# An attention stage that feeds a gated MLP and a second MLP, on one core: query transfers a tile earlier, eight weight conversions moved into attention, mismatch products by column parts, copies dealt out anew

## The chip, the cores and the metric

The kernel runs on one core of a Trainium2 chip. The metric is the device time of one execution in microseconds. Engines are named as in the profile: PE is the matrix engine (PEld its weight loads), DVE, ACT and POOL the vector, scalar and general engines, SP the engine that issues most transfers. Every engine takes its own instructions in order.

## The reference, cut to what matters

```python
# attention, B=2, H=8, S=768, D=64; 6 sign bits of q @ proj and k @ proj give a bucket
q_bits = (q @ proj) > 0 ; k_bits = (k @ proj) > 0
mask   = bucket(q)[..., :, None] == bucket(k)[..., None, :]
scores = where(mask, (q @ k.T) / sqrt(D), -1e9)
attn   = softmax(scores) ; x = (attn @ v) laid out as [B, S, H*D]        # 512 wide
# first MLP
h = relu(x @ w_in) ; u, v = halves(h)                                    # w_in 512 x 1024
v = layernorm(v) ; g = u * (w_spatial @ v + b_spatial)                   # w_spatial 768 x 768
x = g @ w_out                                                            # w_out 512 x 512
# second MLP
out = x + relu((layernorm(x) * g_ln) @ w_ch1) @ w_ch2                    # 512 x 2048, 2048 x 512
```

The weights w_in, w_out, w_ch1 and w_ch2 arrive as 64-bit floats, two 32-bit words to a number.

## The kernel before, in words

**Attention** walks 96 tiles, in the order batch, head, group, tile: a tile is 128 queries against all 768 keys of one head, two tiles make a group, three groups a head, two heads a pair. `attn_step(i)` issues the transposes of tile i, the scores of tile i+2, the maximum (DVE, line 310) and the exponential (ACT, line 323) of tile i+1, and, at each second tile, the product with the values (`weighted`, line 351) of the group that ended two tiles ago. The transposed exponentials leave PSUM in two halves `e`: half c=0 is copied by ACT (line 340), half c=1 by DVE (line 342). `weighted` writes 64 output columns at a time, in turn to the upper and the lower half of the partitions.

**Per pair**, `pair_load` brings raw keys and queries, `mismatch` multiplies them with the signs' projection (PE, line 245, four products of 384 columns with a full 128-wide weight, two instructions each) and DVE turns the sums into mask rows `m` (line 246, two instructions); `pair_split` splits keys and queries into a high and a low part on POOL and DVE; `head_prep` (keys) and `group_prep` (queries) call `passes_of`, which lets SP copy the parts and the mask rows from SBUF to SBUF into the operand tiles `ks` and `qs` (lines 269, 270, 275). These five stand at 10, 7, 6, 4 and 0 tiles ahead of their pair (`AT`); `group_prep` stands `QA` = 3 tiles and one step ahead of its group, with `QB` = 3 buffers.

**Conversion of weights** (`stage_f64`, `words_f64`, `join_f64`, `split_f64`): a 512 KB load issued from ACT's queue, one ACT instruction (line 102), five on DVE (103 to 107), one on POOL (111), and then the split into a high part on ACT (80) and a low part on POOL (86). Twelve such pieces (w_out, then both halves of w_in) are converted during attention at the tiles `CONV_AT`, and stored to DRAM by `kept` for a second use. The other 32 pieces (`w1_piece`, `w2_piece`, sixteen each, names f_w, w1t, w2t) are converted after attention by `load_f64`.

**The first MLP**, `moe1(b)`, runs for batch 0 from tile 60 of attention on, in between the tiles, and for batch 1 after attention, where the list `fill` hangs steps of the second MLP between its steps: pieces 0 to 4 of w1 and w2, layer norms, and `second(0)` to `second(4)`. The rest of the pieces (5 to 15) comes after, two a step of `second`.

**Order.** The order of instructions on each engine is made by the planner of the framework, from a simulated timeline; `tc.issue_after(...)` ties a step to an instruction that must have been issued before it. What the program's order says is thus a start, not the order on the chip.

## Time and profile before

| what | value |
|---|---|
| median of 3 runs | 737.61 us (737.4 to 738.12) |
| the profiled execution's own time | 737.13 us |
| its span, first to last instruction | 734.9 us |
| PE busy | 686.0 us (93%) |
| DVE busy | 438.7 us (60%) |
| ACT busy | 303.6 us (41%) |
| POOL busy | 190.9 us (26%) |
| mean DMA rate | 115 GB/s, 84.37 MB |

How to read it: the shares are means over stages. The profile's own table by slices shows DVE near 90% in the first quarter of the span and again late in the third, and near 15% in the last fifth. The execution that the profile shows took 2.2 us more than its span, and 0.5 us less than the median of the runs.

### The profile page before, as it was taken

What the parts mean: (1) busy time and instruction counts of PE and PEld (TensorE: products, weight loads), DVE (VectorE), ACT (ScalarE), POOL (GpSimd) and SP (SyncE); (2) the same over time, 40 slices, a digit from 0 to 9 for tenths busy, and PEclk for the clock granted to TensorE, in tenths of its full rate; (3) what the DMA queues carried; (4) which work ended last, traced back from release to release, by engine and by line L of the source; (5) the groups of instructions that cost most, each with busy time, mean ns of one, the idle gap of its engine ahead of it and who ended that gap; (6) DMA issues with size and microseconds to landing.
All of it is one profiled execution on the core that took longest, in us unless ns stands there. A gap on an engine that the chain in (4) does not pass through costs nothing.

```text
span 734.9 us, 9990 instructions
## 1 busy us (share of the span) xinstructions
PE 686.0 (93%) x3580; PEld 533.1 (73%) x3580; DVE 438.7 (60%) x849; ACT 303.6 (41%) x583; POOL 190.9 (26%) x182
## 2 busy tenths in 40 slices
PE   6999999898999999998889999799988999999997
PEld 5767667675767777776678887587766788888885
DVE  3698987897665645444798459676899712112112
ACT  2676766685556545344364222453323201100100
POOL 2234143334352222110144243244544400000000
PEclk8899999999999999999999999899999999999999
DMA  6765866674554554212625153523232101001001
GB/s 168 187 159 155 248 163 179 207 195 122 156 175 98 178 179 102 80 38 72 220 62 197 44 165 122 199 90 114 89 112 86 58 1 57 1 0 58 1 0 58
DMA packets 51922, 84.37 MB, mean 115 GB/s; under 512 B 6970, under 2 KB 36206, under 8 KB 50850
## 3 DMA queue, kind: packets, MB, share of 16 engines
q1 hardware_dynamic: 38834, 54.37, 25.8%
q10 hardware_dynamic: 13040, 29.36, 12.3%
q8 instruction: 29, 0.48, 0.3%
q14 instruction: 19, 0.16, 0.1%
HBM read 51.12 MB, written 12.58 MB: 87 GB/s over the span
## 4 chain that ended last, share of the span: by engine, by line
PE 60%; DVE 15%; DMA 11%; ACT 4%; issue 4%; POOL 3%; SPq 1%; DVEq 0%; ACTq 0%; POOLq 0%
PE acc L747 12%; PE pc L437 11%; PE sc L299 7%; DMA f_w<-in_w 7%; PE pv L437 7%; PE pt L337 6%; PE pg L607 6%; PE po L351 6%; PE py L437 3%; POOL f64c_w L111 2%; DVE f_w L105 2%; DVE x L310 2%; DMA qs<-q 2%; DMA f_v<-in_w_in 1%; DVE f64c_w L107 1%
## 5 line engine op out<-in xcount | busy, mean ns | idle before, releaser
L747 PE MATMUL acc<-w2t,ch 128*128 128x512 f32 x576 | 145.3, 398 | 6.6 <-DVE ch L738 5.2
L437 PE MATMUL pc<-xh,w1t 128*128 128x512 f32 x576 | 146.9, 400 | 3.9 <-DVE xh L731 2.7
L747 PEld LDWEIGHTS acc<-w2t,ch 128*128 128x128 f32 x576 | 107.5, 189 | 34.5 <-DVE ch L738 8.1
L437 PEld LDWEIGHTS pc<-xh,w1t 128*128 128x128 f32 x576 | 110.0, 192 | 30.0 <-ACT f64c_w L102 2.9
L310 DVE TENSOR_SCALAR_CACHE_REDUCE x<-sc 128x768 f32<-128x768 f32 x96 | 89.5, 950 | 23.1 <-PE sc L299 22.9
L323 ACT ACTIVATE x<-x,nb 128x768 f32<-128x768 f32 x96 | 89.3, 931 | 32.7 <-DVE x L310 32.6
L738 DVE SCALAR_TENSOR_TENSOR ch<-pc,ch 128x512 fp32r<-128x512 f32 x48 | 33.0, 688 | 112.6 <-ACT ch L737 112.6
L299 PE MATMUL sc<-ks,qs 128*128 128x512 f32 (+3 forms) x384 | 86.3, 363 | 9.2 <-PE po L351 3.1
L337 PE MATMUL pt<-ident,x 128*128 128x128 f32 x576 | 79.8, 278 | 9.8 <-ACT x L323 9.3
L337 PEld LDWEIGHTS pt<-ident,x 128*128 128x128 f32 x576 | 67.6, 143 | 26.7 <-ACT x L323 17.6
L737 ACT ACTIVATE ch<-pc 128x512 fp32r<-128x512 f32 x48 | 28.5, 593 | 131.5 <-PE pc L437 131.5
L299 PEld LDWEIGHTS sc<-ks,qs 128*128 128x128 f32 (+1 forms) x384 | 59.8, 199 | 21.6 <-PE po L351 6.2
L351 PE MATMUL po<-e,vv 128*64 128x256 f32 x576 | 74.1, 393 | 0.4 <-DVE m L246 0.4
L111 POOL TENSOR_TENSOR f64c_w<-f_w,f64c_w 128x512 f32<-128x512 f32 x32 | 43.7, 1368 | 93.9 <-DVE f64c_w L107 77.9
L340 ACT ACTIVATE e<-pt 128x384 f32<-128x384 f32 x96 | 46.5, 488 | 45.4 <-PE pt L337 44.5
L342 DVE COPY e<-pt 128x384 f32<-128x384 f32 x96 | 52.7, 549 | 20.7 <-PE pt L337 20.2
L351 PEld LDWEIGHTS po<-e,vv 128*64 128x64 f32 x576 | 37.5, 138 | 24.4 <-issue 7.3
L102 ACT ACTIVATE f64c_w<-f_w 128x512 f32<-128x512 f32 x32 | 21.4, 669 | 63.0 <-DMA f_w<-in_w 59.6
L607 PE MATMUL pg<-vn,w_sp 128*128 128x512 f32 x180 | 44.1, 397 | 0.0
L437 PE MATMUL pv<-w_u,act_x 128*128 128x512 f32 x144 | 37.8, 398 | 4.7 <-DMA w_u<-ws_u 2.8
L607 PEld LDWEIGHTS pg<-vn,w_sp 128*128 128x128 f32 x180 | 33.3, 188 | 7.6
L437 PE MATMUL py<-w_out,act_g 128*128 128x512 f32 x144 | 35.8, 396 | 2.1 <-ACT act_g L426 2.1
(131 smaller groups left out, 813.3 us busy)
## 6 DMA issues: line engine op xcount, KB each, us to landing
f_w<-in_w ACTq DMA_DIRECT2D x32, 512.0 KB
ks<-k SPq DMA_DIRECT2D x48, 192.0 KB
qs<-q SPq DMA_DIRECT2D x144, 64.0 KB
wst_sp<-in_w_spT SPq DMA_DIRECT2D x12, 384.0 KB
w_out<-ws_out SPq DMA_DIRECT2D x2, 2048.0 KB
vv<-in_v SPq DMA_DIRECT2D x16, 192.0 KB
ot<-y_dram SPq DMA_DIRECT2D x12, 256.0 KB
out<-ot SPq DMA_DIRECT2D x12, 256.0 KB
```

The costliest lines, as they stand in the source:

```text
L111: nc.gpsimd.tensor_tensor(cf, tf, cf, op=ALU.add)
L299: nc.tensor.matmul(sc[:, csl], qs[:rows, i, qsl], ks[:rows, i, csl], start=(i == 0), stop=(i == 1))
L310: last["max"] = nc.vector.tensor_scalar(x, t["sc"], MASKED, FMAX, op0=ALU.min, op1=ALU.min, accum_out=nb,).ins
L323: last["exp"] = nc.scalar.activation(t["x"], t["x"], AF.Exp, bias=t["nb"], scale=-1.0, accum_out=z_sum[b][:, n, h : h + 1]).ins
L337: nc.tensor.transpose(pt[:, i, :], t["x"][:, kt * P : (kt + 1) * P], ident)
L340: nc.scalar.activation(e, pt, AF.Copy)
L342: nc.vector.tensor_copy(e, pt)
L351: nc.tensor.matmul(po[a : a + D, :GW], heads[b, h]["vv"][:, kt], gr["e"][:, kt], start=(kt < 2), stop=(kt >= NKT - 2))
L437: mm = nc.tensor.matmul(ps, lh(i), rh(j), start=(n == 0), stop=(n == tot - 1)).ins
L607: nc.tensor.matmul(pg, w[i][:, k], vn[:, j, k, :], start=(n == 0), stop=(n == len(order3) - 1))
L738: last["lo"] = nc.vector.scalar_tensor_tensor(ch[:, 1], pc, 0.0, ch[:, 0].bitcast(F32), op0=ALU.max, op1=ALU.subtract).ins
L747: last["mm"] = nc.tensor.matmul(accs[c][t], ch[:, i, t * P : (t + 1) * P], w2t[f][:, j, 0, :], start=(start and n == 0), stop=(stop and n ...
```

## The change

- `QA` and `QB` go from 3 to 4: `group_prep` is called a tile sooner, and `qs` has a fourth buffer.
- `passes_of` for queries copies the high part into both of its places by one transfer that repeats its source, so a group has three transfers in place of four. Keys keep three, and their mask rows come in two transfers in place of one, since `m` is now laid out otherwise.
- `mismatch` makes eight products of 256 columns with a 32-wide weight in place of four of 384 with a 128-wide one. Each writes 32 partitions of its own: keys of columns 0 to 511, keys of 512 to 767, and the same of the queries. One DVE instruction over 512 columns makes all mask rows, in place of two over 384. The third 256 columns are computed twice. Constants `sides`, `above` and `worth` follow (POOL, at the start).
- Half c=1 of `e` is copied by ACT in place of DVE in batch 0 for the second tile of each group.
- `CONV_AT` gets eight more tiles, 62 to 90, and `conversions` eight more pieces: w1 and w2 of f = 0 to 3 (`NS` = 4). Each is stored to DRAM by `kept`; `w1_piece` and `w2_piece` then load the converted piece with SP in place of `load_f64`.

```diff
-    CONV_AT = (5, 9, 14, 19, 24, 29, 34, 39, 44, 49, 53, 57)
+    CONV_AT = (5, 9, 14, 19, 24, 29, 34, 39, 44, 49, 53, 57, 62, 66, 70, 74, 78, 82, 86, 90)
+    NS = 4
-    QA = 3
-    QB = 3
+    QA = 4
+    QB = 4
...
-        m = ap.tile([P, S], F32R, tag="m", name=f"m_{b}_{r}", bufs=2)
-        for c in range(2):
-            csl = slice(c * KC, (c + 1) * KC)
-            pm = ps_b.tile([P, 512], F32, tag="b", name=f"pm_{b}_{r}_{c}")
-            for i, nm in enumerate("kq"):
+        m = ap.tile([P, 2 * GW], F32R, tag="m", name=f"m_{b}_{r}", bufs=2)
+        pm = ps_b.tile([P, 2 * GW], F32, tag="b", name=f"pm_{b}_{r}")
+        for half in range(2):
+            for n, (nm, g) in enumerate((("k", half), ("k", 2), ("q", half), ("q", 2))):
                 raw = pairs[b, r][nm, "raw"]
-                nc.tensor.matmul(pm[:, :KC], side[nm], raw[:, csl], start=(i == 0), stop=(i == 1))
-            nc.vector.tensor_scalar(m[:, csl], pm[:, :KC], above, worth, op0=ALU.is_gt, op1=ALU.mult)
+                out_n = pm[n * QUAD : (n + 1) * QUAD, half * GW : (half + 1) * GW]
+                nc.tensor.matmul(out_n, side[nm], raw[:, g * GW : (g + 1) * GW], start=True, stop=True)
+        nc.vector.tensor_scalar(m, pm, above, worth, op0=ALU.is_gt, op1=ALU.mult)
...
-        for a in range(2):
-            nc.sync.dma_start(out=t[a * D : (a + 1) * D, 0].bitcast(F32), in_=two[own, a, sl])
-        nc.sync.dma_start(out=t[0:D, 1].bitcast(F32), in_=two[own, 1 - LOW[nm], sl])
...
+        if nm == "k":
+            for a in range(2):
+                nc.sync.dma_start(out=t[a * D : (a + 1) * D, 0].bitcast(F32), in_=two[own, a, sl])
+            nc.sync.dma_start(out=t[0:D, 1].bitcast(F32), in_=two[own, 1, sl])
         else:
-            nc.sync.dma_start(out=t[D:MR, 1].bitcast(F32), in_=rows)
+            nc.sync.dma_start(out=t[0:D].bitcast(F32), in_=two[own, 0:1, sl].to_broadcast([D, 2, n]))
+            nc.sync.dma_start(out=t[D:P, 0].bitcast(F32), in_=two[own, 1, sl])
+        for lo, hi in ((0, 2 * GW), (2 * GW, S)):
+            lo, hi = max(sl.start, lo), min(sl.stop, hi)
+            if lo < hi:
+                at = (2 * "kq".index(nm) + lo // (2 * GW)) * QUAD + h % 2 * HROW
+                rows = pr["m"][at : at + NM, lo % (2 * GW) : lo % (2 * GW) + hi - lo].bitcast(F32)
+                to = t[D:MR, 1, lo - sl.start : hi - sl.start]
...
-            if c == 0:
+            if c == 0 or (b == 0 and j == 1):
                 nc.scalar.activation(e, pt, AF.Copy)
...
+        for f in range(NS):
+            for key, src, shape in (
+                ("w1", w1[:, :, f * P : (f + 1) * P], [P, 2, KFT, P]),
+                ("w2", w2[:, f : f + 1, :], [P, 2, 1, DM]),
+            ):
+                def dst(key=key, f=f, shape=shape):
+                    return ap.tile(shape, F32R, tag="early", name=f"early_{key}_{f}", bufs=2)
+                def after(to, key=key, f=f, shape=shape):
+                    kept(f"{key}_{f}", shape, to)
+                res.append(converted(src, dst, f"{key}_{f}", after))
...
-        load_f64(w1t[f][:, 0], w1t[f][:, 1], w1[:, :, f * P : (f + 1) * P], f"w1_{f}")
+        if f < NS:
+            nc.sync.dma_start(out=w1t[f].bitcast(F32), in_=w_split[f"w1_{f}"])
+        else:
+            load_f64(w1t[f][:, 0], w1t[f][:, 1], w1[:, :, f * P : (f + 1) * P], f"w1_{f}")
```

`w2_piece` is changed as `w1_piece` is.

## Rows read from the trace of the kernel before

**Rows 1.** Windows by stage; columns: window, length, busy (count) PE PEld DVE ACT POOL, clock, DMA share, GB/s
```profile
0.00:184.00 184.00, 163.66 (x1071) 121.03 (x1072) 144.28 (x305) 116.75 (x241) 60.61 (x79) 0.96 0.65 178
184.00:347.00 163.00, 159.12 (x935) 122.38 (x933) 87.52 (x190) 82.99 (x167) 37.75 (x33) 1.00 0.41 118
347.00:484.00 137.00, 125.42 (x562) 99.64 (x562) 99.18 (x204) 54.18 (x93) 43.05 (x32) 0.96 0.42 143
484.00:584.00 100.00, 92.23 (x387) 72.12 (x387) 81.78 (x114) 33.01 (x55) 48.00 (x37) 0.98 0.31 95
```
**Rows 2.** Waits of PE, 20 to 184 us; columns: total us, times, longest
```profile
PE pt L337 <- ACT x L323: 9.3, 10, 2.1
```
**Rows 3.** Windows, two pairs of heads in batch 0
```profile
64.60:96.60 32.00, 29.75 (x209) 21.84 (x207) 29.87 (x62) 22.19 (x48) 12.53 (x12) 1.00 0.64 189
96.60:128.00 31.40, 29.69 (x209) 21.92 (x207) 24.99 (x55) 20.85 (x45) 10.63 (x11) 1.00 0.69 180
```
**Rows 4.** Timeline of PE, 63 to 67 us; columns: start, us, instructions
```profile
63.10 1.52 PE L351 MATMUL po<-e,vv 128*64 128x256 f32 x12
64.55 0.91 PE L245 MATMUL pm<-k,sides 128*128 128x384 f32 x2
65.30 0.81 PE L245 MATMUL pm<-q,sides 128*128 128x384 f32 x2
65.94 0.81 PE L245 MATMUL pm<-k,sides 128*128 128x384 f32 x2
```
**Rows 5.** Line 351 by itself: duration ns min/median/max, and idle time before it
```profile
L351 PEld LDWEIGHTS po<-e,vv x576: 132/137/230, 27.2 to 348.9; 128*64 128x64 f32 x192
...
  issue: 7.3, 37
```
**Rows 6.** Groups by line; columns: count, busy us, mean ns, idle before
```profile
L342 DVE COPY e<-pt 128x384 f32<-128x384 f32 x96 | 52.7, 549 | 20.7 <-PE pt L337 20.2
L340 ACT ACTIVATE e<-pt 128x384 f32<-128x384 f32 x96 | 46.5, 488 | 45.4 <-PE pt L337 44.5
L246 DVE TENSOR_SCALAR m<-pm,above,worth 128x384 fp32r<-128x384 f32 x16 | 10.4, 668 | 3.0 <-PE pm L245 2.9
```
**Rows 7.** Windows, tile f64c_w alone, whole span; busy (count) DVE, ACT, POOL
```profile
0.00:735.00 735.00, 105.06 (x160) 41.52 (x64) 85.60 (x64) 0.98 0.39 115
```
**Rows 8.** Waits of ACT, 33 to 184 us, those of the conversions
```profile
ACT f64c_v L102 <- DMA f_v<-in_w_in: 4.9, 4, 3.1
ACT w_out L80 <- POOL f64c_out L111: 3.3, 1, 3.3
```
**Rows 9.** Timeline of ACT, 206 to 214 us; in brackets the idle time before
```profile
212.49 0.67 ACT L102 ACTIVATE f64c_w<-f_w 128x512 f32<-128x512 f32 x1 [5.61 <-DMA f_w<-in_w]
```
**Rows 10.** Timeline of PE at the same place
```profile
214.06 2.11 PE L437 MATMUL pv<-w_u,act_x 128*128 128x512 f32 x8 [1.24 <-DVE xT L358]
```
**Rows 11.** Waits of PE, 345 to 480 us
```profile
PE pv L437 <- DMA w_u<-ws_u: 2.8, 1, 2.8
PE pc L437 <- DVE xh L731: 2.7, 1, 2.7
PE px_c L728 <- DVE mv L167: 2.2, 1, 2.2
...
PE ptr_g L424 <- DVE gt L609: 1.8, 1, 1.8
PE pv L437 <- ACT vr L531: 1.5, 1, 1.5
```
**Rows 12.** Timeline of SP at the start
```profile
7.48 2.13 SPq L269 DMA_DIRECT2D qs<-q  x2
9.66 0.59 SPq L270 DMA_DIRECT2D qs<-q  x1
```
**Rows 13.** Timeline of PE at the start
```profile
13.27 2.90 PE L299 MATMUL sc<-ks,qs 128*128 128x512 f32 x8 [3.09 <-DMA qs<-q]
```
**Rows 14.** Waits in SP's queue, whole span
```profile
SPq L269 <- PE pt L337: 29.9, 22, 4.1
```

More of the change, by code (lines that the diff above doesn't have):

```diff
@@ L132, in attn_moe_kernel @@
     nc.sync.dma_start(out=pj, in_=proj.rearrange("(o d) n -> o d n", o=1).to_broadcast([2, D, NB]))
-    K_FROM, Q_FROM = 38, 0
-    M_AT = {"k": (D, NB), "q": (D + 32, 32 + NB)}
-    sides = const.tile([P, K_FROM + P], F32, name="sides")
+    HROW = 3 * NB
+    QUAD = 32
+    sides = const.tile([P, NB + QUAD], F32, name="sides")
     nc.gpsimd.memset(sides, 0.0)
-    for own, at in zip((slice(0, D), slice(D, P)), M_AT["q"]):
+    for a, own in enumerate((slice(0, D), slice(D, P))):
         for i, sign in enumerate((1.0, -1.0, 1.0)):
-            nc.gpsimd.tensor_scalar(
-                sides[own, at + i * NB : at + (i + 1) * NB], pj[own], sign, 0.0, op0=ALU.mult, op1=ALU.add
-            )
-    side = {"k": sides[:, K_FROM : K_FROM + P], "q": sides[:, Q_FROM : Q_FROM + P]}
+            at = a * HROW + i * NB
+            nc.gpsimd.tensor_scalar(sides[own, at : at + NB], pj[own], sign, 0.0, op0=ALU.mult, op1=ALU.add)
+    side = {"k": sides[:, NB : NB + QUAD], "q": sides[:, 0:QUAD]}
     above = const.tile([P, 1], F32, name="above")
     worth = const.tile([P, 1], F32, name="worth")
-    for t, fills in (
-        (above, ((0, P, 0.0), (0, NM, -TINY), (32, NB + NM, -TINY), (32, NM, 0.0), (D, NB, -TINY))),
-        (above, ((D + 32, NM, -TINY), (D + 32, NB, 0.0))),
-        (worth, ((0, P, 1.0), (32, NB + NM, MASKED), (D + 32, NM, MASKED))),
-    ):
-        for at, n, value in fills:
-            nc.gpsimd.memset(t[at : at + n], value)
+    nc.gpsimd.memset(above, 0.0)
+    nc.gpsimd.memset(worth, 1.0)
+    for at in range(0, P, QUAD):
+        keys = ((4 * NB, -TINY), (3 * NB, 0.0), (NB, -TINY))
+        queries = ((5 * NB, -TINY), (4 * NB, 0.0), (2 * NB, -TINY), (NB, 0.0))
+        for n, value in keys if at < 2 * QUAD else queries:
+            nc.gpsimd.memset(above[at : at + n], value)
+    nc.gpsimd.memset(worth[2 * QUAD : P], MASKED)
     b_sb = const.tile([P, NQT], F32, name="b_sb")
@@ L264, in passes_of @@
         pr = pairs[b, h // 2]
[L265 removed]
         two = pr[nm].bitcast(F32)
         own = slice(h % 2 * D, (h % 2 + 1) * D)
[L268 to L275 removed]
+        if nm == "k":
+            for a in range(2):
+                nc.sync.dma_start(out=t[a * D : (a + 1) * D, 0].bitcast(F32), in_=two[own, a, sl])
+            nc.sync.dma_start(out=t[0:D, 1].bitcast(F32), in_=two[own, 1, sl])
+        else:
+            nc.sync.dma_start(out=t[0:D].bitcast(F32), in_=two[own, 0:1, sl].to_broadcast([D, 2, n]))
[6 more added lines that the diff above has]
+                to = t[D:MR, 1, lo - sl.start : hi - sl.start]
+                if first:
+                    nc.vector.tensor_copy(to, rows)
+                else:
+                    nc.sync.dma_start(out=to.bitcast(F32), in_=rows)
         return t
@@ L696, in w2_piece @@
         w2t[f] = pool.tile([P, 2, 1, DM], F32R, tag=f"w2_{slot}", name=f"w2t_{f}", bufs=1)
-        load_f64(w2t[f][:, 0], w2t[f][:, 1], w2[:, f : f + 1, :], f"w2_{f}")
+        if f < NS:
+            nc.sync.dma_start(out=w2t[f].bitcast(F32), in_=w_split[f"w2_{f}"])
+        else:
+            load_f64(w2t[f][:, 0], w2t[f][:, 1], w2[:, f : f + 1, :], f"w2_{f}")
     def x_tile(c):
```

5 lines of the change are left out of this document (1 added, 4 removed).

## The prediction

> **What bounds the kernel now.** I read the windows by stage first [rows 1], because the shares of the whole span hide the stages. In attention with batch 0 and the start of batch 1 (0 to 184 us) PE is busy 163.7 of 184 us and DVE 144.3. From 184 to 347 us, where the first MLP of batch 0 runs between the tiles, PE is busy 159.1 of 163 us and DVE only 87.5: PE alone is the bound there. From 347 to 484 us PE stands idle for 137 - 125.4 = 11.6 us at a clock of 0.96, from 484 to 584 us for 7.8 us while DVE, busy 81.8 of 100, converts weights. The last 150 us, which the change doesn't touch, are matmuls alone.
>
> In the first stage PE's waits come next: most of what the profile names there is one wait, the transposes on the exponentials, 9.3 us in ten pieces [rows 2]. That looks like DVE being too busy, since the exponential waits for the maximum that DVE makes. Two pairs show how far this carries [rows 3]: one has 29.9 us of DVE work in 32.0 us, the next 25.0 in 31.4. Five microseconds less of DVE brought 0.6 us, because PE is busy for 29.7 us in either. So PE is the bound in batch 0 too, with DVE close behind; work taken off PE counts in full, work taken off DVE for about an eighth.
>
> **The change part by part.** The sum is made against the profiled execution's 737.1 us, 0.5 below the median of the runs.
>
> *Column parts.* A pair's mismatch is eight PE instructions of 384 columns; two of them take 65.94 - 65.30 = 0.64 us, so 0.32 each, 2.56 us in all, 0.83 ns a column [rows 4]. The new form has 16 instructions of 256 columns (eight products of two instructions) at 32-wide weights. No row shows four parts side by side; the nearest is the product with the values, which alternates two 64-wide parts: 12 instructions of 256 columns from 63.10 to 64.55, 0.121 us each where a lone one would take 0.83 x 256 = 0.213. Bounds: 16 x 0.213 = 3.41 us if nothing overlaps; 16 x 0.121 = 1.93 if four overlap like two; half of that, 0.97, if four overlap twice as well. Four parts are nearer to the lower two, I take 1.4. Weight loads idle 7.3 us in 37 places ahead of the value products [rows 5], 0.2 us for each change from full to divided weights; the mismatch adds one such change, so 1.6 us. Saved: 1.0 us a pair, on seven pairs (the first pair's lies beside the start's transfers): **-6.7 us** (from -11.1 to +7.4). The Trainium skill (TensorEngine Tiling (Array Packing), Key Properties) says that changing the tiling mode drains the engine; the 0.2 us agree with a drain, and without it the sum would be 1.4 us better.
>
> *Copies and mask rows.* In batch 0, 24 of the 96 copies of 549 ns leave DVE and become 24 of 488 ns on ACT [rows 6]: -13.2 us of DVE, +11.7 us of ACT. The mask's two instructions of 668 ns [rows 6] become one of 512 columns, between 0.67 and 1.34 us, say 0.8: -0.5 us of DVE a pair. A pair in batch 0 thus has 3.9 us less on DVE and 2.9 us more on ACT, some 26 and 25 us of 31, both below PE. By the eighth from rows 3 that is 0.5 us a pair; by the waits [rows 2] it could be all 9.3. I take 0.75 us on four pairs: **-3 us** (0 to -9.3; +4 if the exponentials now queue behind copies).
>
> *Queries' transfers.* PE's list of waits after the start holds no wait for queries at all [rows 2, 11], though SP's own queue waits 29.9 us in 22 places for a buffer to come free [rows 14]. A fourth buffer removes part of those waits and hurries transfers that nobody waits for: **0**. The cover is the lead of four tiles, about 10 us at 32 us for 12 tiles. What the step is moved past: all three transfers of a pair's first group now stand between the split and the keys' transfers in SP's queue. If POOL has not finished the split, SP stands until it has, and behind it stand that pair's keys and values and whatever SP stores for the first MLP. They are due four tiles later, so a stand of 2 or 3 us is hidden; it would cost its whole length only with less than that left. Keys issue one transfer more a head, queries one less a group (48 less against 16 more), so SP gets lighter.
>
> *Start.* PE's first scores wait 3.09 us for queries [rows 13]; SP issues high part, low part, and the high part again, 0.59 us last [rows 12]. That last one goes: **-0.6 us** (0 to -1). Seven more small fills on POOL lie under the wait for the first keys: 0.
>
> *Eight conversions in attention.* 32 conversions cost DVE 105.1, ACT 41.5 and POOL 85.6 us [rows 7], each 3.3, 1.3 and 2.7. Eight add 26 us of DVE, 10 of ACT and 22 of POOL to a stage of 163 us where these are busy 87.5, 83.0 and 37.8 [rows 1]. There is room on each; the price is order, since ACT stands at the load's landing, at POOL's join, and at POOL's low part before the store. For the twelve conversions in batch 0 the two largest entries of such stands are 4.9 and 3.3 us [rows 8], 0.7 us each; with smaller ones I take 1 us. What a stand passes on to PE one place shows: ACT stood 5.6 us for a weight piece [rows 9] and PE then idled 1.24 us [rows 10], a fifth. Eight conversions with 1 us of stand pass on about 2 us: **+2 us** (0, if PE's moe products cover all, to 8 x 1.24 = 10). Eight stores and loads of 0.5 MB add to a DMA share of 0.41 there: hidden.
>
> *After attention.* DVE loses 8 x 3.3 = 26 us between 347 and 470 us, and ACT and POOL their parts. Of PE's waits there [rows 11] those behind a crowded DVE or ACT (gt 1.8, vr 1.5) should go, 3.3 us; those on the second MLP's layer norm (2.2 and 2.7) have no conversion ahead of them but come behind the same queue, and the wait for the reloaded w_u (2.8) may grow as the converted pieces use the same queue and DMA engines. I take **-4 us** (+3, if that reload's wait doubles, to -8.2). From 484 to 584 us pieces 5 to 15 are converted as before, into space that the first MLP frees: 0.
>
> Sum: -0.6 - 6.7 - 3 + 2 - 4 = -12.3; 737.1 - 12.3 = 724.8, so **725 us**.
>
> **The rivals.** *Larger gain:* four parts overlap fully (-11.1), all waits on exponentials go (-9.3), all of DVE's share after attention (-8.2): 737.1 - 0.6 - 11.1 - 9.3 - 8.2 = 708. For it speaks the DVE at 93% in one pair, against it the pair at 80% that is as long [rows 3]. Chance 0.19.
>
> *The parts don't overlap:* each pair costs 3.41 + 0.2 instead of 2.56, +7.4 in place of -6.7, and the time is 725 + 14 = 739. Chance 0.06, since the value products do overlap. The Trainium skill (TensorE: Matmul & The Clock Gate, Part 3: Packing small matmuls) says that a weight load overlaps running products only where the row group differs, and here all four parts have the same rows; by that rule this is what comes. The trace goes against it: value products follow each other at 0.121 us though one load lasts 0.137 [rows 4, 5].
>
> *Slower: ACT is held up in the second batch.* If each new conversion stands ACT as long as the one of rows 9, and half of it instead of a fifth comes through to PE, which has its products in one queue behind the transposes, eight cost 8 x 2.8 = 22 us in place of 2: 745. It decides from 8 x 1.8, that is from 1.8 us a conversion on. For it: the store's stand ends with POOL, which makes the MLP's low parts too; against it: a tile there takes 163 / 36 = 4.5 us, so the load, issued a tile ahead, has longer to land than in batch 0. Chance 0.14.
>
> *Nothing comes through:* savings on PE are filled by waits that were hidden behind it, and the gain after attention is used up by the layer norm's chain: 737 (736 to 738.5). Chance 0.06.
>
> **How the numbers follow.** Forecast 0.55, with a range of its own of 717 to 732; 0.19, 0.06, 0.14 and 0.06 for the rivals. The range 708 to 741 holds forecast, larger gain, no overlap and no change in the main, and the lighter part of the slower case. A difference of 0.2% (1.5 us) is about what can be told from none. Faster: 0.55 + 0.19 = 0.74; same: 0.06 and half of no overlap, 0.09; slower: 0.17.
>
> **What would show it.** Right: mismatch instructions of 256 columns about 0.09 us apart; pairs in batch 0 of 30 us or a little more; PE's idle time between 184 and 347 us below 6 us in spite of 26 us more of DVE; waits for gt and vr gone after attention; the stretch from 484 us on as long as before. Wrong: those instructions 0.2 us apart; ACT's stands at line 102 or at the store followed by idle PE; a longer wait for w_u.

## The result, and the profile after

The changed kernel takes 742.9 us (median of 17 runs, 738.3 to 749.8) and the kernel before, on the same chip, 737.4 (17 runs): a ratio of 1.0083 with a 95% interval of 1.0063 to 1.0103. It is slower, and outside the range of 708 to 741. In the experiments below, the profiled executions of a_cb2 and p_conv2 ran at a granted clock of 0.75; they are not read, and the medians and ratios below leave them out.

The windows by stage of the changed kernel (its profiled execution: 746.0 us, a span of 744.2) stand against [rows 1]:

```profile
0.00:184.00 184.00, 161.58 (x1102) 117.77 (x1104) 125.15 (x265) 121.57 (x259) 59.84 (x82) 0.93 0.63 173
184.00:347.00 163.00, 154.64 (x925) 118.75 (x922) 116.90 (x232) 89.61 (x180) 65.24 (x53) 0.98 0.53 164
347.00:484.00 137.00, 125.53 (x572) 99.14 (x571) 73.93 (x151) 45.84 (x80) 16.65 (x15) 0.97 0.40 143
```

Work moved as the change says: from 184 to 347 us DVE has 29.4 us more, from 347 to 484 us 25.3 us less. But PE's idle time in the second stage rose from 3.9 to 8.4 us, and behind attention it stayed as it was (11.5 after 11.6). The granted clock, the third figure from the end, fell from 0.96 to 0.93 in the first stage and from 1.00 to 0.98 in the second.

Where the time went is read by comparing the start of the same piece of work in both traces. Counted from 0, the columns are value products 9, 18 and 24 (24 is the first of batch 1), 33, 35 and 47 (the last) of both batches, then two of the first MLP of batch 1 (pv 16 and pg 9) and the last product of the kernel. Each entry is the start minus that in the kernel before, in us:

```
place in before   75.7  121.5  156.5  224.8  241.8  347.1  367.3  432.5  726.7
after             +5.2   +8.8   +4.6   +3.6   +9.5   +9.6  +12.4  +11.5   +9.3
```

Three losses stand out: up to 8.8 us within batch 0, half of which a stall of the kernel before (134 to 140 us) gives back; 5.8 us between 225 and 242 us; and 2.8 us at 367 us, so that nothing at all is gained behind attention.

*Batch 0.* The mismatch of the third pair in PE's timeline; it answers to [rows 4]:

```profile
72.91 0.41 PE L247 MATMUL pm<-k,sides 128*32 128x256 f32 x2
72.92 0.41 PE L247 MATMUL pm<-q,sides 128*32 128x256 f32 x2
...
73.91 0.55 PE L347 MATMUL pt<-ident,x 128*128 128x128 f32 x3
```

Sixteen instructions take 73.91 - 72.91 = 1.00 us, 0.06 us each, where eight took 2.56; all seven pairs after the first are alike. They run side by side: the keys' part and the queries' part start 0.01 us apart. PE's waits from 20 to 184 us, against [rows 2]:

```profile
PE pt L347 <- ACT x L333: 4.7, 7, 2.2
PE po L361 <- ACT e L350: 3.9, 2, 2.8
PE sc L309 <- issue: 2.7, 1, 2.7
PE pt L347 <- ACT e L350: 1.7, 1, 1.7
```

The wait on exponentials is halved, from 9.3 us; in its place stand waits for copies on ACT (3.9 and 1.7 us) and one at the scores. The one at the scores comes first in time. POOL's timeline shows where it starts:

```profile
35.27 0.86 POOL L229 TENSOR_SCALAR q<-q 128x768 fp32r<-128x768 f32 x1 [9.10 <-DMA q<-in_qT]
36.08 2.86 POOL L87 TENSOR_TENSOR k<-k 128x384 fp32r<-128x384 f32 x2
```

and PE's timeline where it ends:

```profile
41.86 2.90 PE L309 MATMUL sc<-ks,qs 128*128 128x512 f32 x8 [2.69 <-issue]
```

The queries split at 35.27 belong to the pair after next. POOL waits 9.1 us for them while the low part of the next pair's keys stands behind them; before, the two halves of that low part came first (34.08 and 35.30) and the later queries last (37.04). The keys' low part is done 2.4 us later (38.94 us against 36.50), and PE stands at the pair's first scores. This order on POOL is not the whole loss of batch 0, though. a_noconv (below) has it too, with no stand of more than 0.5 us at these scores, and is 7.0 us behind at 121.5 us; a_cb2_again has it, stands 1.72 us, and is 4.9 us ahead.

The other four of PE's waits above 1 us between 20 and 184 us (1.68, 2.22, 1.16 and 2.76 us, at 67.8, 98.6, 130.3 and 161.1 us) each lie behind a stand of ACT for a conversion's load (2.41, 2.56, 1.38 and 2.90 us), with copies or exponentials queued after it. The last of them, in ACT's timeline and in PE's:

```profile
159.85 0.66 ACT L103 ACTIVATE f64c_u<-f_u 128x512 f32<-128x512 f32 x1 [2.90 <-DMA f_u<-in_w_in]
```

```profile
161.08 2.83 PE L361 MATMUL po<-e,vv 128*64 128x256 f32 x12 [2.76 <-ACT e L350]
```

Of this kind the kernel before and a_cb2_again have none above 1 us. So the waits for copies are no price of the moved copies alone: the slower rival's mechanism is at work in batch 0 already, with the twelve old conversions.

*The clock.* A stand costs more than its length. The 12 value products at 161.08 take 2.83 us, those of [rows 4] 1.52, because the granted clock there is 0.50, which is 1.2 in place of 2.4 GHz; the window:

```profile
161.10:163.90 2.80, 2.80 (x13) 1.27 (x14) 0.75 (x2) 2.14 (x5) 0.00 (x0) 0.50 0.92 351
```

The six longest stands of PE from 20 to 347 us (2.69, 1.68, 2.22, 2.76, 2.42 and 3.09 us) are each followed by such a stretch. In windows of 1 us PE is at 1.2 GHz for 28 of these 327 us, in the kernel before for 6. An estimate from PE's busy time in these windows is that half speed costs 13.6 us, against 2.9 before. These 10.7 us more are as much as the column parts save, and more than the idle time that PE gained (5.9 us). The trace is no exception: the mean clock is 0.962 to 0.973 in all 17 runs, and 0.977 to 0.988 in those of the kernel before that stand beside the experiments.

*At 240 us.* ACT's timeline:

```profile
239.88 0.63 ACT L81 ACTIVATE early_w<-f64c_w 128x512 fp32r<-128x512 f32 x1 [2.24 <-POOL f64c_w L112]
239.94 0.39 ACTq L94 DMA_DIRECT2D f_w<-in_w  x1
...
243.79 0.66 ACT L103 ACTIVATE f64c_w<-f_w 128x512 f32<-128x512 f32 x1 [2.90 <-DMA f_w<-in_w]
244.35 0.92 ACT L333 ACTIVATE x<-x,nb 128x768 f32<-128x768 f32 x1
```

and PE's:

```profile
245.42 0.88 PE L347 MATMUL pt<-ident,x 128*128 128x128 f32 x6 [3.09 <-ACT x L333]
```

ACT first stands 2.24 us for POOL's join, then issues the next piece's load and stands 2.90 us until it lands; the exponential is behind it in the queue, and PE idles 3.09 us. It is the mechanism of the slower rival, in one place of eight.

*Behind attention.* PE's waits from 345 to 480 us, against [rows 11]:

```profile
PE pv L447 <- DMA w_u<-ws_u: 4.4, 1, 4.4
...
PE ptr_g L434 <- DVE gt L633: 0.5, 1, 0.5
```

The waits for vr (1.5) and nearly that for gt (1.8 to 0.5) are gone, as forecast; that for w_u has grown. ACT's and SP's timelines, the window from 365 to 375 us and PE's timeline show what stands around it:

```profile
360.40 1.05 ACTq L94 DMA_DIRECT2D f_w<-in_w  x2
362.37 0.32 SPq L530 DMA_DIRECT2D w_u<-ws_u  x1
...
364.44 1.07 SPq L717 DMA_DIRECT2D w1t<-ws_w  x1
```

```profile
365.00:375.00 10.00, 5.57 (x20) 4.23 (x20) 7.20 (x19) 2.90 (x5) 0.71 (x1) 0.88 1.00 372
```

```profile
372.57 4.56 PE L447 MATMUL pv<-w_u,act_x 128*128 128x512 f32 x12 [4.43 <-DMA w_u<-ws_u]
```

Two loads of the next pieces (1 MB) are issued just ahead of w_u (2 MB), and four of the eight converted pieces (2 MB) are reloaded behind it, all issued by 366.58 us; the DMA share is 1.00 from 365 to 375 us. The loads ahead go with the longer wait, and not the reloads behind: in all eight kernels read here that have the two loads there, the products start 10.1 to 11.2 us after w_u's issue, also in b_pad and p_q, which reload no converted piece; in the ten that do not, 8.0 to 8.8 us after it.

The 12 products that follow take 4.56 us. Those of the kernel before, and of p_parts, at this place:

```profile
361.77 2.99 PE L437 MATMUL pv<-w_u,act_x 128*128 128x512 f32 x12 [2.79 <-DMA w_u<-ws_u]
```

```profile
357.52 4.56 PE L442 MATMUL pv<-w_u,act_x 128*128 128x512 f32 x12 [2.63 <-DMA w_u<-ws_u]
```

p_parts has none of these transfers (DMA share 0.36 from 357.6 to 362 us) and the same 4.56 us. The clock makes the difference: its mean is 0.62 over these products there and in the changed kernel, and 1.00 in the kernel before.

### The profile page after: what moved, and what is told of

Same layout as the page of the kernel before. It is cut to its first block, busy times and chain, and to the rows that moved or that the text cites. A ratio compares the mean times of both kernels' runs of the same rounds, so it can differ in the third digit from the quotient of the medians.

```text
span 744.2 us, 10044 instructions
## 1 busy us (share of the span) xinstructions
PE 687.8 (92%) x3644; PEld 532.4 (72%) x3644; DVE 433.0 (58%) x818; ACT 310.7 (42%) x607; POOL 195.9 (26%) x189
## 4 chain that ended last, share of the span: by engine, by line
PE 46%; DMA 18%; DVE 14%; issue 11%; POOL 5%; ACT 5%; SPq 2%; ACTq 0%; DVEq 0%; POOLq 0%
PE acc L777 11%; PE pc L447 10%; DMA f_w<-in_w 7%; PE sc L309 5%; PE po L361 4%; PE pt L347 4%; PE pv L447 4%; PE pg L631 3%; PE py L447 3%; POOL f64c_w L112 2%; DMA f_u<-in_w_in 2%; DVE f_w L106 2%; DMA f_v<-in_w_in 2%; DVE x L320 2%; DMA w_u<-ws_u 1%
## 5 line engine op out<-in xcount | busy, mean ns | idle before, releaser
L320 DVE TENSOR_SCALAR_CACHE_REDUCE x<-sc 128x768 f32<-128x768 f32 x96 | 89.7, 949 | 29.4 <-PE sc L309 29.2
L309 PE MATMUL sc<-ks,qs 128*128 128x512 f32 (+3 forms) x384 | 88.0, 370 | 10.8 <-issue 4.7
L347 PE MATMUL pt<-ident,x 128*128 128x128 f32 x576 | 81.4, 282 | 10.3 <-ACT x L333 7.8
L361 PE MATMUL po<-e,vv 128*64 128x256 f32 x576 | 76.5, 403 | 4.3 <-ACT e L350 3.9
L350 ACT ACTIVATE e<-pt 128x384 f32<-128x384 f32 x120 | 56.1, 487 | 37.0 <-PE pt L347 35.8
L352 DVE COPY e<-pt 128x384 f32<-128x384 f32 x72 | 39.6, 551 | 20.0 <-PE pt L347 19.6
L447 PE MATMUL pv<-w_u,act_x 128*128 128x512 f32 x144 | 40.8, 422 | 6.9 <-DMA w_u<-ws_u 4.4
L103 ACT ACTIVATE f64c_w<-f_w 128x512 f32<-128x512 f32 x32 | 21.4, 672 | 56.1 <-DMA f_w<-in_w 49.6
L447 PEld LDWEIGHTS pv<-w_u,act_x 128*128 128x128 f32 x144 | 28.7, 204 | 15.3 <-issue 5.6
```

The lines of the kernel that those rows point to most:

```text
L309: nc.tensor.matmul(sc[:, csl], qs[:rows, i, qsl], ks[:rows, i, csl], start=(i == 0), stop=(i == 1))
L320: last["max"] = nc.vector.tensor_scalar(x, t["sc"], MASKED, FMAX, op0=ALU.min, op1=ALU.min, accum_out=nb,).ins
L347: nc.tensor.transpose(pt[:, i, :], t["x"][:, kt * P : (kt + 1) * P], ident)
L350: nc.scalar.activation(e, pt, AF.Copy)
L352: nc.vector.tensor_copy(e, pt)
L361: nc.tensor.matmul(po[a : a + D, :GW], heads[b, h]["vv"][:, kt], gr["e"][:, kt], start=(kt < 2), stop=(kt >= NKT - 2))
```

## The experiments

All are compared with the kernel before on the same chip. First all results; the offsets are at the places of the table above.

```
kernel        median   ratio [95%]               121.5  156.5  224.8  241.8  347.1  367.3  726.7
p_parts       734.5    0.9953 [0.9930, 0.9976]    -1.6   -4.0   -4.3   -3.3   -3.8   -2.7   -2.0
p_copies      740.3    1.0054 [1.0032, 1.0075]    +1.5   -0.3   +0.2   +0.3   +0.4   -1.0   +1.5
p_conv        745.5    1.0119 [1.0083, 1.0156]    +0.8   -0.7   +1.7   +3.3   +4.5   +8.7  +11.6
p_q           744.1    1.0113 [1.0067, 1.0160]    +6.0   +4.2   +3.7   +3.7   +3.9  +10.1  +11.3
q_qa          736.7    0.9970 [0.9947, 0.9994]    -0.6   -0.9   -1.9   -1.9   -2.0   -3.7   -3.2
b_pad         743.4    1.0089 [1.0053, 1.0125]    +1.1   +0.7   +0.7   +0.7   +0.9  +11.8  +11.5
q_merge       754.0    1.0221 [1.0182, 1.0261]    +9.7   +9.6  +11.6  +11.6  +11.5  +12.8  +18.3
q_hold        745.2    1.0103 [1.0071, 1.0134]    +8.9   +5.8   +6.8   +6.8   +7.1   +6.3   +7.1
a_nomerge     745.7    1.0122 [1.0085, 1.0160]    -0.8   -0.6   +2.1   +6.2   +7.2  +10.4   +7.8
a_noconv      735.8    0.9972 [0.9944, 1.0000]    +7.0   +3.0   +1.2   +2.2   +0.9   +0.2   +2.2
a_cb2         727.7    0.9870 [0.9832, 0.9909]
a_cb2_again   728.9    0.9872 [0.9818, 0.9926]    -4.9   -9.8  -12.5  -12.5   -8.9   -6.8   -5.8
a_e1          745.6    1.0101 [1.0042, 1.0160]    +3.4   -0.3   -1.8   +5.2   +5.8   +7.7  +11.5
b_cb2         739.3    1.0032 [1.0003, 1.0062]    +1.9   +2.2   +1.8   +1.8   +1.6   -0.2   +0.0
best          734.7    0.9965 [0.9939, 0.9991]    +0.0   -0.8   -1.3   -0.3   -1.9   -3.1   -2.7
best_cb2      726.9    0.9863 [0.9821, 0.9905]    -0.1   -1.4   -7.7   -7.7   -9.5   -9.7  -10.3
c2_best       727.8    0.9858 [0.9816, 0.9899]    -4.1   -6.4  -12.0  -12.1  -13.2   -9.3  -11.9
p_conv2       745.0    1.0102 [1.0031, 1.0172]
```

### One part at a time

**p_parts**: the kernel before with the column parts alone (the change's `sides`, `above`, `worth`, `mismatch` and the mask rows in `passes_of`), of which the core is:

```diff
-            for i, nm in enumerate("kq"):
+            for n, (nm, g) in enumerate((("k", half), ("k", 2), ("q", half), ("q", 2))):
                 raw = pairs[b, r][nm, "raw"]
-                nc.tensor.matmul(pm[:, :KC], side[nm], raw[:, csl], start=(i == 0), stop=(i == 1))
+                out_n = pm[n * QUAD : (n + 1) * QUAD, half * GW : (half + 1) * GW]
+                nc.tensor.matmul(out_n, side[nm], raw[:, g * GW : (g + 1) * GW], start=True, stop=True)
```

> The kernel before with the column parts of the mismatch alone (new layout of m, mask rows of the keys in two transfers; queries keep four transfers, three buffers). Theory A, that PE's saved time counts: in the changed kernel the sixteen instructions took 1.0 us where eight took 2.56, so with six to seven pairs on the path this kernel is 7 to 10 us faster than before, 728 to 731. Theory B, that what is saved on PE is taken up by stalls that were hidden behind it: within 2 us of before.

Faster by 0.5%, some 3.4 us, between the two theories. PE saves 7 x 1.56 = 10.9 us. Its wait on exponentials [rows 2] shrinks too, but others come in its place, from 20 to 184 us:

```profile
PE pt L342 <- ACT x L328: 4.0, 6, 1.6
PE sc L304 <- issue: 3.4, 2, 1.9
PE sc L304 <- DMA ks<-m: 1.8, 1, 1.8
```

The scores now wait for keys and their mask rows. PE's idle time from 20 to 184 us is all the same no longer than before (12.6 us after 13.7). What is lost shows elsewhere: from 184 to 347 us PE idles 8.6 us, before 3.9, and in both stages together it is at 1.2 GHz for 13 us, before 6.

**p_copies**: the copies alone.

```diff
-            if c == 0:
+            if c == 0 or (b == 0 and j == 1):
```

> The kernel before with the 24 copies dealt to ScalarE alone. Theory A, VectorE relieved: 2 to 4 us faster. Theory B, ScalarE's queue is what the transposes wait for and 11.7 us more in it delay exponentials: 2 to 6 us slower. Theory C, PE alone bounds batch 0: within 1 us.

Slower by 0.5%. PE's waits from 20 to 184 us:

```profile
PE pt L337 <- ACT x L323: 4.3, 6, 1.6
PE sc L299 <- issue: 4.0, 1, 4.0
PE po L351 <- ACT e L340: 3.8, 4, 1.7
```

The wait on exponentials shrinks by 5.0 us, and the value products now wait 3.8 us for copies on ACT. ACT, not DVE, has become late, and not by copies alone: the two longest of the four waits (1.66 and 1.48 us) lie behind stands of ACT for a conversion's load (1.49 and 1.57 us). The profiled execution (offset +1.5 at the end) does not show the 4 us of the median at one place, so where the rest goes stays open.

**p_conv**: the eight conversions alone (`CONV_AT`, `NS`, the loop in `conversions`, the reloads in `w1_piece` and `w2_piece`).

```diff
-    CONV_AT = (5, 9, 14, 19, 24, 29, 34, 39, 44, 49, 53, 57)
+    CONV_AT = (5, 9, 14, 19, 24, 29, 34, 39, 44, 49, 53, 57, 62, 66, 70, 74, 78, 82, 86, 90)
+    NS = 4
```

> The kernel before with the eight conversions in attention alone. Theory A, that ScalarE is held up in the second batch by the conversions' loads and joins, and that nothing comes back after attention: 5 to 10 us slower than before, with the loss between 215 and 260 us. Theory B, that the loss there is bad luck of one plan: within 3 us of before. The forecast's own terms: 2 us lost in attention, 4 gained behind it, so 2 us faster.

Slower by 1.2%: 5 us in attention and 7 behind it. Behind attention PE's wait is the one for w_u, and ACT stands for weight pieces; PE's waits from 345 to 480 us, then ACT's:

```profile
PE pv L438 <- DMA w_u<-ws_u: 5.1, 1, 5.1
```

```profile
ACT f64c_w L103 <- DMA f_w<-in_w: 11.2, 3, 6.9
```

**a_noconv**: the changed kernel with the twelve conversions of before.

```diff
-    CONV_AT = (5, 9, 14, 19, 24, 29, 34, 39, 44, 49, 53, 57, 62, 66, 70, 74, 78, 82, 86, 90)
-    NS = 4
+    CONV_AT = (5, 9, 14, 19, 24, 29, 34, 39, 44, 49, 53, 57)
+    NS = 0
```

> The changed kernel without the eight conversions in attention (they are made after it, as before). The fourth buffer's 2 KB and the smaller mask rows' 2 KB cancel, and the loads of w1 and w2 come at about 200 us again. Theory A (conversions hold ScalarE up, and the place of memory loses the early loads): 6 to 10 us faster than the changed kernel, 733 to 738. Theory B (the copies and the queries' step lose the time in batch 0): within 3 us of the changed kernel.

By the ratios it gives 8 us back. The loss in batch 0 is still there (+7.0 at 121.5 us), those at 240 us and behind attention are gone: these two belong to the conversions, with the memory that they take.

### The queries' transfers taken apart

**p_q**: the kernel before with the merged transfer (its diff is at q_merge) and

```diff
-    QA = 3
-    QB = 3
+    QA = 4
+    QB = 4
```

> The kernel before with the queries' step a tile sooner, the fourth buffer and the merged transfer alone. Theory A, nobody waits for these transfers: within 1.5 us of before. Theory B, the step now stands ahead of the keys' transfers and the split, and scores wait for keys, as at 39 us of the changed kernel: 2 to 6 us slower, with idle PE ahead of scores in batch 0.

Slower by 1.1%, for a step that the prediction puts at 0. The next three take it apart.

**q_qa**: begun a tile sooner, nothing else.

```diff
-    QA = 3
+    QA = 4
```

> The kernel before with the queries' step a tile sooner, three buffers and four transfers a group. Theory A (place of memory): within 2 us of before, since the loads stay at 198 us. Theory B (the step stands ahead of the split and of the keys' transfers in SP's queue): 3 to 5 us slower, lost in batch 0, as in the kernel with all three edits of the queries.

Faster by 0.3%. This part is harmless.

**b_pad**: the kernel before with an unused tile of 2 KB a partition in attention's pool, the size of the fourth query buffer. Nothing reads it; POOL fills one column of it.

```diff
+    spare = ap.tile([P, GRP * GW], F32, tag="spare", name="spare", bufs=1)
+    nc.gpsimd.memset(spare[:, 0:1], 0.0)
```

> The kernel before with 2 KB a partition of unused memory in attention's pool and nothing else (a fourth buffer of queries takes as much). Theory A, that the fourth buffer costs by its place: the memory of the conversions' buffers after attention moves onto tiles that live to the end of attention, so the first two loads of w1 and w2, issued at 198 us before, come only at about 350 us, beside the reload of w_u, and ScalarE stands for them. Then this kernel is as before to 347 us and 4 to 7 us slower in all. Theory B, that the fourth buffer's cost is in attention: within 1.5 us of before.

Slower by 0.9%, all of it between 347 and 367 us (the profiled execution, with 748.2 us the longest of six, shows 10.9 us there). ACT's timeline shows the first loads of the first MLP pieces (w1_0 and w2_0) and what follows; before, they were issued at 198.29 us and stood in [rows 9] at 212:

```profile
351.78 1.44 ACTq L93 DMA_DIRECT2D f_w<-in_w  x2
355.65 0.66 ACT L102 ACTIVATE f64c_w<-f_w 128x512 f32<-128x512 f32 x1 [0.80 <-DMA f_w<-in_w]
364.64 0.66 ACT L102 ACTIVATE f64c_w<-f_w 128x512 f32<-128x512 f32 x1 [7.22 <-DMA f_w<-in_w]
```

PE's waits from 340 to 400 us:

```profile
PE pv L437 <- ACT xT L582: 5.8, 1, 5.8
PE pv L437 <- DMA w_u<-ws_u: 5.4, 1, 5.4
```

With 2 KB less, these loads move from the second batch to behind attention, into the reload of w_u; ACT stands 7.22 us for one of them, and xT, which PE waits for, comes later in its queue, behind a further stand of 2.16 us. The 12 products after either wait take 5.46 and 5.43 us in place of 3.0, at 1.2 GHz: by PE's busy and idle time from 347 to 400 us, about half of the loss is waits and half is the clock. What a buffer costs here is not its use but its place. Why 2 KB change the order of ACT's queue the trace does not show. In the changed kernel the first pieces that are not converted in attention are loaded at 360 us, in the same place.

**q_merge**: three transfers in place of four, nothing else.

```diff
-        for a in range(2):
-            nc.sync.dma_start(out=t[a * D : (a + 1) * D, 0].bitcast(F32), in_=two[own, a, sl])
-        nc.sync.dma_start(out=t[0:D, 1].bitcast(F32), in_=two[own, 1 - LOW[nm], sl])
+        if nm == "k":
+            for a in range(2):
+                nc.sync.dma_start(out=t[a * D : (a + 1) * D, 0].bitcast(F32), in_=two[own, a, sl])
+            nc.sync.dma_start(out=t[0:D, 1].bitcast(F32), in_=two[own, 1, sl])
+        else:
+            nc.sync.dma_start(out=t[0:D].bitcast(F32), in_=two[own, 0:1, sl].to_broadcast([D, 2, n]))
+            nc.sync.dma_start(out=t[D:P, 0].bitcast(F32), in_=two[own, 1, sl])
```

> The kernel before with the merged transfer of the queries alone. Theory A, one issue less a group is worth at most the 0.6 us at the start: 0 to 1 us faster. Theory B, a transfer that reads its source twice lands later and scores wait for it: 2 to 4 us slower, lost in batch 0.

Slower by 2.2%, the worst of all and far beyond either theory, in many small steps. POOL's timeline from 30 to 42 us:

```profile
32.98 1.01 POOL L86 TENSOR_TENSOR k<-k 128x384 fp32r<-128x384 f32 x1 [7.85 <-PE pm L245]
36.49 0.91 POOL L228 TENSOR_SCALAR q<-q 128x768 fp32r<-128x768 f32 x1 [2.50 <-DVE xT L362]
37.37 1.69 POOL L86 TENSOR_TENSOR k<-k 128x384 fp32r<-128x384 f32 x1
```

The later pair's queries have moved between the halves of the key's low part, as in the changed kernel they moved ahead of both. Since a_noconv and a_cb2_again show that order without a loss at the scores, why the merged transfer costs 2.2% alone stays open.

**q_hold**: q_merge with one buffer in place of two for a pair's queries.

```diff
-            pr[nm] = ap.tile([P, 2, S], F32R, tag=nm + "2", name=f"{nm}2_{b}_{r}", bufs=1 if nm == "k" else 2)
+            pr[nm] = ap.tile([P, 2, S], F32R, tag=nm + "2", name=f"{nm}2_{b}_{r}", bufs=1)
```

> The kernel before with the merged query transfer, and one buffer in place of two for a pair's queries, so that the next pair's load and split can't be begun before the last group of the pair has been sent. Theory (order on POOL: the merged transfer lets the next pair's query split come before the second half of the key's low part, keys arrive late and PE stands at the scores): the two halves of the key's low part follow each other again, PE's idle time at the scores of 39 to 42 us goes, and the run gains most of the 16 us back: 737 to 744 us. Rival (the merged transfer itself is slow, or arrives later than two): the order is restored but the time stays at 750 to 757. A cost of its own that this kernel may have: the split of the next pair's queries comes later and its mismatch with it, up to 8 us, visible as a wait for queries at the pair's first scores.

Some 9 us better than q_merge, but the edit brings a wait of its own, so it decides nothing. POOL's timeline:

```profile
37.70 1.03 POOL L228 TENSOR_SCALAR q<-q 128x768 fp32r<-128x768 f32 x1 [11.21 <-DMA ks<-k]
```

The queries of the next pair itself now wait 11.2 us for the one buffer, with the key's low part behind them (38.70 us).

**a_nomerge**: the changed kernel with four transfers, the diff of q_merge the other way round.

> The changed kernel with four separate query transfers in place of three. If the merged transfer costs there what it costs alone (16 us): 727 us. If it costs what the offsets of the changed kernel against the one before show by place (8.7 us at 95 to 126 us, 2 us of them left at 152): 735 to 741, with the second pair's scores of 39 to 47 us back on time and the second batch begun 2 us sooner. If the cost lies in memory's place and in the conversions alone: 742 to 744, no change.

Batch 0 loses nothing any more (-0.8 in place of +8.8 at 121.5 us), so the merged transfer has a part in that loss; but a_cb2_again has the merged transfer and does not lose there either (-4.9), so the loss takes the single conversion buffer as well. At 156.5 us only 5 us of the difference are left, the stalls at 240 us and behind attention come as before, and the time is that of the changed kernel. A gain in batch 0 is not kept there.

### The single conversion buffer

**a_cb2**: the changed kernel with two buffers for a conversion's words in attention, and one for the converted pieces, for which there is no more space.

```diff
-    CB0 = 1
+    CB0 = 2
-                    return ap.tile(shape, F32R, tag="early", name=f"early_{key}_{f}", bufs=2)
+                    return ap.tile(shape, F32R, tag="early", name=f"early_{key}_{f}", bufs=1)
```

> The changed kernel with two buffers in place of one for the words of a conversion in attention (and one in place of two for the converted pieces, since no more space is left). Theory (the single buffer makes ScalarE issue the next load only when the join has read it, so that ScalarE stands for the load's landing and exponentials queue behind, 4.3 us of PE between 200 and 290 us): the stall at 240 us goes, 738 to 741. Rival (the piece's load is late for want of DMA engines, whatever the buffers): the stand stays, 742 to 746. The loss behind attention stays in either.

1.3% faster than before and, by the ratios, some 16 us below the changed kernel, where the theory gave it 2 to 5. **a_cb2_again** is the same kernel, measured once more; **a_e1** makes the second half of the edit alone, **b_cb2** gives the kernel before the second buffer.

> The kernel with two conversion buffers in attention once more, for an execution at full clock: the one profiled before ran at a granted clock of 0.75 and its trace can't be set against the others. If the gain of 1.3% against the kernel before is real, 726 to 731 us. If ScalarE's stands were the cause: PE's idle time between 184 and 347 us falls from 8.4 to below 5 us, the stall at 240 us is gone, and the loads of w1_0 to w2_3 are issued one to two tiles ahead of their absolute value. If instead the gain lies behind attention: the second batch ends as late as in the changed kernel and 347 to 484 us are shorter.

> The changed kernel with one buffer in place of two for the converted pieces in attention, and still one conversion buffer. It separates the two halves of the edit of the kernel with two conversion buffers. If the second conversion buffer is what helped: 742 to 746 us, like the changed kernel. If the single buffer of the converted pieces (the store of one must be done before the next is written, and 12 KB of memory less) is what helped: 727 to 733.

> The kernel before with two conversion buffers in attention in place of one, and nothing else. If ScalarE's stands for a conversion's load cost the kernel before too (its twelve conversions in batch 0 show stands of 4.9 and 3.3 us): 728 to 733 us, and the gain belongs to the buffer and not to the change. If the gain needs the eight conversions in the second batch, where the stand at 240 us was: 736 to 741; a loss to 744 if the 12 KB of the buffer move the first loads of the later weights behind attention as the 2 KB alone did.

The gain is real (0.9872 again), it is the second conversion buffer's (a_e1 stays at 1.0101), and the kernel before has no use for that buffer (1.0032). ACT's waits for conversions' loads in batch 0 (33 to 184 us), in the changed kernel:

```profile
ACT f64c_out L103 <- DMA f_out<-in_w_out: 5.8, 4, 2.4
ACT f64c_v L103 <- DMA f_v<-in_w_in: 5.3, 3, 2.6
ACT f64c_u L103 <- DMA f_u<-in_w_in: 4.4, 2, 2.9
```

and in a_cb2_again:

```profile
ACT f64c_v L103 <- DMA f_v<-in_w_in: 3.2, 3, 1.6
ACT f64c_u L103 <- DMA f_u<-in_w_in: 2.7, 4, 1.1
ACT f64c_out L103 <- DMA f_out<-in_w_out: 2.1, 2, 1.4
```

15.5 us become 8.0 (9.5 in the kernel before). With one buffer a piece's load can be issued only when the join has read the piece before. Of the step at 240 us nothing is left (-12.5 at 225 and at 242 us). The expectation looked for the effect there, but 14.4 us lie in batch 0, whose end comes that much sooner than in the changed kernel (-9.8 against +4.6); the second batch adds to it, and behind attention some is lost again. From 20 to 184 us PE idles 2.9 us less than in the changed kernel and is at 1.2 GHz for 5.5 us in place of 21.4, which by the estimate above is worth 7.9 us. That the second buffer brings the gain is shown by these four runs; that it does so through ACT's stands, earlier loads and the clock is read from the traces, and that the planner's other order of instructions has a part in it is not excluded.

**best** and **best_cb2**: column parts and `QA = 4` (three query buffers, four transfers, twelve conversions, copies as before), with one conversion buffer and with two. best_cb2 against best:

```diff
-    CB0 = 1
+    CB0 = 2
```

> The kernel before with the column parts and the queries begun a tile sooner (QA = 4), with three query buffers, the four separate transfers, no conversions in attention beyond the twelve, no copies moved. If the gains of the two edits add (0.9953 and 0.9970 alone): 0.992, some 731.5 us. If the stalls that took most of the column parts' gain are stalls that the earlier transfers remove (waits for queries and keys): more, 0.985 to 0.99, 726 to 730. If both edits hit the same limit (the chain of the exponentials): 0.995 to 0.997, 733 to 735.

> The kernel before with column parts, queries begun a tile sooner and two conversion buffers; no conversions beyond the twelve, no copies moved, three query buffers, four transfers. Two conversion buffers alone gave 1.0032 and these two edits without them 0.9965. If the second buffer is what lets the time saved on PE in batch 0 come through (ScalarE no longer stands for a piece while exponentials queue), the first batch ends 7 to 10 us sooner than before and the time is 727 to 731 us, the conversions in the second batch adding nothing. If the gain needs the eight conversions in attention (27 us less of VectorE's work behind it): 733 to 738.

0.9965 and 0.9863, as expected in time but not in place: the first batch ends 1.4 us sooner than before, not 7 to 10, and the gain comes between 156.5 and 224.8 us (-1.4 to -7.7). The second buffer, worth nothing to the kernel before, is worth 1% once PE's work is shorter. The last load of the twelve conversions in ACT's timeline of best, and in that of best_cb2 (186.32 us in the kernel before):

```profile
200.42 0.34 ACTq L93 DMA_DIRECT2D f_u<-in_w_in  x1
```

```profile
169.24 0.34 ACTq L93 DMA_DIRECT2D f_u<-in_w_in  x1
```

The window from 184 to 347 us of best, and of best_cb2:

```profile
184.00:347.00 163.00, 156.40 (x952) 118.62 (x951) 91.04 (x192) 82.98 (x167) 40.94 (x35) 1.00 0.42 124
```

```profile
184.00:347.00 163.00, 160.41 (x969) 122.94 (x968) 87.88 (x185) 82.78 (x167) 33.47 (x30) 0.99 0.43 127
```

With one buffer the twelve conversions end later, not sooner, when PE is faster, and run into the second batch, where PE idles 6.6 us; with two they end 31 us sooner and PE idles 2.6.

**c2_best** and **p_conv2**: a_cb2 without the merged transfer and the moved copies (the diffs of q_merge and p_copies the other way round); and p_conv with the diff of a_cb2.

> The kernel with two conversion buffers, with four separate query transfers and without the copies moved to ScalarE: column parts, queries a tile sooner, four query buffers, eight conversions. If the merged transfer and the copies cost there what they show alone (16 and 4 us): 709 to 715. If they cost half, as the offsets by place show for the merged transfer: 718 to 724. If two conversion buffers already hide what they cost: 726 to 731, and against the kernel before 0.985 to 0.99.

> The kernel before with the eight conversions in attention and two conversion buffers (one buffer for the converted pieces), nothing else. With one conversion buffer they cost 1.2%. If the single buffer was their whole price: 1.003 or less, 731 to 740 us. If most of the price lies behind attention, where the first loads of the later pieces meet the reload of w_u: 742 to 746, and the offset against the kernel before grows after 347 us.

c2_best (0.9858) and best_cb2 (0.9863) can't be told apart: the eight conversions and the fourth query buffer bring nothing that best_cb2 has not. Without the column parts the conversions cost 1.0% with two buffers as they cost 1.2% with one. a_cb2 (0.9870) can't be told from c2_best either, so with the second buffer the merged transfer and the moved copies cost little or nothing. c2_best, too, has two loads of later pieces just ahead of w_u; it waits 4.90 us for w_u and loses 3.9 of its 13.2 us there.

## Why the prediction was wrong

The step that failed is the one that the whole sum rests on, that work taken off PE counts in full and that what is added to ACT, SP and POOL hides beside it. Term by term:

*Column parts* (-6.7): the mechanism was right and the size on PE larger, 7 x 1.56 = 10.9 us, the far end of its range. The sentence of the Trainium skill (TensorE: Matmul & The Clock Gate, Part 3: Packing small matmuls) that the rival draws on speaks of weight loads, that they overlap running products only where the row group differs; the rival took it to mean that nothing overlaps. The trace decides against both, with 0.06 us an instruction, all on the same rows, though a weight load lasts 0.11. What failed is that time taken off PE counts in full: alone the parts bring 3.4 us, with a second conversion buffer and the earlier queries 10. The two pairs of [rows 3] were read for DVE only. The chain of conversions through ACT, DVE and POOL has a pace of its own, set by its single buffer, and was not in the sum; nor was PE's clock, whose fall after the longest stands cost as much as the parts saved.

*Copies and mask rows* (-3): the mask instruction takes the 0.80 us forecast. The copies cost 4 us alone; the end of the range, exponentials and value products queued behind ACT, is what came, in good part behind ACT's stands for loads.

*Queries' transfers* (0): this step failed by 8 us (p_q). It asked only who waits for queries, and q_qa shows that to be nobody. It did not price the fourth buffer's 2 KB (b_pad: +0.9%) nor that a pair's queries released sooner let POOL take the later pair's split first (q_merge: +2.2%). That POOL's order is the cause of q_merge's loss is not shown: q_hold could not show it, and a_noconv and a_cb2_again have that order without such a loss at the scores.

*Start* (-0.6): the first scores start at 14.19 us in place of 13.27; the first value product at the same time as before. Nothing gained.

*Eight conversions* (+2): 5 us in attention (p_conv, which with the next term makes +9 us of a forecast -2); in the changed kernel one stand at 240 us, with 5.8 us between 225 and 242. The load's longer time to land was no cover, since with one buffer the load is issued late. The fifth of a stand that comes through to PE rested on one place, where PE was released by DVE [rows 9, 10]; at 240 us a stand of 2.90 us was followed by 3.09 us of idle PE, and then by the lower clock.

*After attention* (-4): DVE lost the 25 us, gt and vr went, and the clause "the wait for the reloaded w_u may grow" took it all: 2.8 to 4.4 us, with the lower clock behind it. The cause was not the one named there, the converted pieces, but the later pieces' first loads, which now come just ahead. The reload's price was bounded at 3 us; p_conv and b_pad show 7 and 11 us behind attention.

Of the rivals, ACT held up in the second batch came nearest (745), for a part of its reason; that its number fits is luck, since one stand in the second batch and not eight came through, and the rest was lost elsewhere. The parts don't add: p_parts, p_copies, p_conv and p_q sum to +2.4%, together they give +0.8%.

## What to carry to other kernels

Before counting time saved on the busiest engine, look for chains beside it whose pace a single buffer sets: here a second conversion buffer was worth nothing before the change and 1% after it. A buffer, a merged transfer or a load a tile sooner is not free because nobody waits for it; ask what else becomes free sooner and moves ahead in a queue, and what the memory it takes pushes elsewhere. Loads that can wait should not be issued just ahead of one that the critical path waits for. And read the clock column beside the idle time: a stand of the matrix engine can cost a second time, in slow products behind it.

## What the runs showed of the hardware

Four products on 32 columns each, with fp32 data of 256 columns, ran side by side: 1.00 us for 16 instructions, against 1.93 us if four parts overlapped only like the two of the value products. The starts of four instructions lie within 0.02 us, and the next four follow after 0.2 us; at either border of such a group of 16 the step is 0.31 us. An estimate from these steps is 0.1 us for each change of mode, and thus 0.2 us for both borders; the prediction took 0.2 us from [rows 5]. It held that to agree with the Trainium skill (TensorEngine Tiling (Array Packing), Key Properties), by which changing the tiling mode drains the engine; that the longer step is a drain no row shows.

After the six longest stands of PE in attention the granted clock was 0.50 (1.2 GHz) for a while, and 12 value products took 2.83 us in place of 1.52. Two loads of 0.5 MB issued just ahead of a reload of 2 MB went with 10.1 to 11.2 us from its issue to the products that need it, against 8.0 to 8.8 without them.
